# Channel mix of an RWKV layer in six blocks of 512 tokens instead of eight of 384, with one pool of 4 KB buffers and a new plan

## Chip, core and metric

One NeuronCore of a Trainium2 chip runs the whole program. The metric is the time of one execution on the device in microseconds (us). Engines are named as in the profile: PE is TensorE (PEld its weight loads), DVE is VectorE, ACT is ScalarE, POOL is GpSimd, SP is SyncE, whose queue issues every DMA here.

## The reference, cut to what matters

There are 4 batches of 768 tokens and 8 heads of 48 channels, so 384 channels in all.

```python
for t in range(S):                                   # attention, per batch and head
    y[t] = r[t] @ (state + (u * k[t]) v[t]^T)
    state = w[t][:, None] * state + k[t] v[t]^T
x = y as (batch, 768 tokens, 384 channels)
h = (x^T @ U @ V)^T                                  # token mix: 768 -> rank 32 -> 768, over the tokens of a batch
u = x + h
out = u + max(u @ w_ch1, 0) @ w_ch2                  # channel mix: 384 -> 1536 -> 384, each token by itself
```

The token mix needs every token of a batch. The channel mix needs one token at a time, once the token mix of its batch is there.

## The kernel before, in words

**Recurrence.** Each batch is cut into 6 chunks of 128 tokens, 24 in all (`chunk`, L332). A chunk loads the decays (LW), r and k with channels on the partitions (LRK), v (LV) and, after the first batch, r and k with tokens on the partitions (LKR). VectorE scans the decays (F L370, Q L383, with the reciprocal R between them); r and k are scaled by them (RP L390, KS L395, on VectorE or GpSimd). TensorE makes the scores (AM L503), VectorE merges them with the diagonal (CP L506; the diagonal comes by RK L416, RU L419, RED L423 and SEL L433 or L435; in batch 0 by PR L451, MD L457 and DV). TensorE then makes the output (YA L571 and L581, YZ L594 and L598) and adds to the state (DS L513; ZA L542 and ZM L551 carry it on). For DS, k has to be turned: for chunks 0 to 11 TensorE turns it (KT L485) and ScalarE copies it back (KN L494); for chunks 12 to 23 VectorE turns it in 32x32 blocks (KD, L626 by `turn_blocks`, four steps of four instructions). In the same way x is turned for the token mix: by TensorE and ScalarE (XT L654, XN L658) for chunks 0 to 17, by VectorE (XD, L626) for chunks 18 to 23. `TURN_K_DVE` and `TURN_X_DVE` (L36) name the chunks.

**Weights.** `split_raw` (L240) brings 27 pieces of U, V, w1 and w2 in as 64-bit words and turns each into a high and a low fp32r part: AB and E on ScalarE, C1, C2, C3 on VectorE (L286, L293, L300), ADD on GpSimd (L307), then HI and SUB (L317, L324).

**Token mix** (`token_mix`, L666) waits for all six turned chunks of a batch: GA L676, G4, SELM L687, GS, GSL L696.

**Channel mix.** `make_u` (L713) adds the token mix (HP L726 on TensorE, UADD L730 on VectorE) and splits u into high and low (UH L735, UL L741). `ffn` (L759) runs over blocks of `TB` = 384 tokens, two to a batch, eight in all. For each block there are 12 UP steps (L774), each nine matmuls into one PSUM buffer (high and low weight on high u, high weight on low u, for three channel tiles), and after each the split HH (L781 or L783) and HL (L787). Then come 12 DN steps (L810) of nine matmuls, four for each of three output tiles, the sum O (L825) on VectorE and the store OUT (L829). The whole FFN is 8 x 24 x 9 = 1,728 matmuls with 384 columns.

**Buffers.** Hidden activations have a pool of their own (24 tiles of 1.5 KB per partition, 12 pairs), so have the raw weight pieces, which share theirs with u (7), `rk` (4), `kr` (2) and `A` (2). PSUM has three one-bank buffers for the channel mix (`psF`).

**Order.** The steps run in the order of a planner's string, `ORDER` (L53): three digits name a step, its engine where it has two, and a number of leading matmuls (`lead`, L185: bf16 matmuls of 384 columns on constants, issued ahead of the step's own). Each engine's queue holds its steps in this order. `caps` (L219) tells `plan` how many buffers of each pool may be held at one time.

```python
    caps = dict(w=W_BUFS, rk=RK_BUFS, kr=KR_BUFS, v=2, F=2, Q=1, A=2, dv=2, kn=2, Z=2, tr=1, aps=1, y=1, dS=1, ffn=3, xT=3, xn=NCH,
                hid=12, raw=RAW_BUFS, turning=TURNING, cva=CVA_BUFS, g4=1, gs=1, qd=1)
```

Of the kernel before, what the change touches and what calls it, by code (L numbers as in the profile page):

```python
# [27 lines left out]
TB = 384  # L28
RANK = 32
# [10 lines left out]
def channel_order():  # L40
# [49 lines left out]
    "0Fz0Je0F+0F-0Gw0JC0Gt0Jg0Gx0Gu0Ft1Gy0Gv1G+0Ct0Gz1G-"  # L90
    "0Cr0H00K30Cu0Cs0H10Jf0Jv0Cv0KP0Jw1Cw0Jx0J+1KQ1Jy0Cz0Cx0Jz1KR0K60Cy0C+0KS0G00K70G30K80G11C-"
    "0G40K90G50D00G20G60D10D20G90G71G80Ga0GA0IH0GB0II0Il0IJ0Im0Ja1JO0GC0JD0KN0IK0In0Jb0JE1Jh0GF0GD0Io0Ji0GG0KU0JF"
    "0KZ0GH0JG0Ip0K41Ju0GI0Jj0JH0Iq0K50Jl0JI0GJ0Jm0GK0Ka0KO0Ir0KA0Kb1KT0GL0JJ0GE0Gb0GM0JK0GN0GO0JL0KB0GR0GP0GQ0Jk"
    "0GU0IL0GS1Gc0GT0GV1GW0GX0Kc0GY0GZ0KC0Kd0Gd0KD0KE0Gg0Ge0Gf0Gh0Gi0Gj0Gm0Gk0Gl0Gn0H20H50H30H40Go0H61H70Gp0H80Gq"
    "0Gr0HB0H90HA0HE0HC1Jn0Jo0HH0HD0Jp0HK0HF1HI0Jq0KF0HG0HL0HJ0HM0KG0Jr0HN0KH0KI0HQ0HO1KJ0HT0HP0HR0KK0HW0HS0HU1KL"
    "0HZ0HX0HV0HY0Ke0Ha0Hb0Kf0Kl0Kg0Hc0Kh0Ki0Hd0Kj0He0Kk0Km0Hf0Kn0Hi0Hg0Hh0Ko0Hj0Kp0Kq0Kr0Kv0Hk0Ks0Kw0Kt0Kx1Ku0Kz"
    "0Hl0K+0Ky1K-0L00Ho0Hm0Hn0Lt0Lx0Hp0Lu0Ly0Lv0Lw1Lz0L10L+1L-"
    "0Hq0L21M00L30M10Hr0M20L40Hs0Ht0L70L51L60LA0L81L90Lb0LB1LC0LD0LG0LE1LF0LJ0LH0LI0LM0LK1LL0Lc0LN0LO0LP0LS0LQ0LR"
    "0LV0LT1LU0LY0LW1LX0Ld0LZ1La0Le0Lh0Lf0Lg0Li0Lj0Lk0Ln0Ll0Lm0Lo0Lp0M30M60M40M50Lq0M71M80M90Lr0Ls0MC0MA1MB0Md0MD"
    "0ME0MF0MI0MG0MH0ML0MJ0MK0Me0MM1MN0MO0MR0MP1MQ0MU0MS0MT0MX0MV1MW0Ma0MY0MZ0Mf0Mb0Mc0Mg0Mj0Mh0Mi0Mk0Ml0Mm0Mp0Mn"  # L100
    "0Mo0Mq0Mr0Ms0Mt0Mu0"
# [52 lines left out]
def rwkv_moe_kernel(ctx, tc, wT, rkT, vN, rkN, uB, uT, uD, U, V, w1, w2, out):  # L154
# [9 lines left out]
    hidp = pool("hidp", 24)  # L164
# [20 lines left out]
    def lead(to):  # L185
        if leading[0]:
# [32 lines left out]
    caps = dict(w=W_BUFS, rk=RK_BUFS, kr=KR_BUFS, v=2, F=2, Q=1, A=2, dv=2, kn=2, Z=2, tr=1, aps=1, y=1, dS=1, ffn=3, xT=3, xn=NCH,  # L219
                hid=12, raw=RAW_BUFS, turning=TURNING, cva=CVA_BUFS, g4=1, gs=1, qd=1)  # L220
# [802 lines left out]
```

## Time and profile before

| what | value |
|---|---|
| median of 3 runs (lowest, highest) | 488.96 us (488.14, 490.3) |
| profiled execution: its span, from the first to the last instruction | 488.5 us |
| PE busy, share of the span | 456.0 us, 93% |
| DVE busy | 372.3 us, 76% |
| ACT busy | 178.6 us, 37% |
| POOL busy | 120.3 us, 25% |
| DMA moved | 47.38 MB, mean 97 GB/s |
| mean granted TensorE clock | 0.959 |

The profile gives no time for the profiled execution other than its span; the span lies within the runs and 0.5 us under their median. Busy time of an engine is the union of its instructions. In the digit rows of the page, each digit is the busy share of one fortieth of the span in tenths. A matmul's record lasts longer than the distance from one matmul to the next, since matmuls overlap in the array; the pace is the distance between starts.

### The profile page before, as it was taken

What the parts mean: (1) busy time and instruction counts of PE and PEld (TensorE: products, weight loads), DVE (VectorE), ACT (ScalarE), POOL (GpSimd) and SP (SyncE); (2) the same over time, 40 slices, a digit from 0 to 9 for tenths busy, and PEclk for the clock granted to TensorE, in tenths of its full rate; (3) what the DMA queues carried; (4) which work ended last, traced back from release to release, by engine and by line L of the source; (5) the groups of instructions that cost most, each with busy time, mean ns of one, the idle gap of its engine ahead of it and who ended that gap; (6) DMA issues with size and microseconds to landing.
All of it is one profiled execution on the core that took longest, in us unless ns stands there. A gap on an engine that the chain in (4) does not pass through costs nothing.

```text
span 488.5 us, 9955 instructions
## 1 busy us (share of the span) xinstructions
PE 456.0 (93%) x4003; PEld 410.9 (84%) x4003; DVE 372.3 (76%) x768; ACT 178.6 (37%) x471; POOL 120.3 (25%) x110
## 2 busy tenths in 40 slices
PE   7489898899999998999999999999999999999994
PEld 3368665888999977999998779988998899999994
DVE  7798999899989999999998799899328654413410
ACT  5576878466352733445232631150002120100100
POOL 2526533543355262650400312020000010000000
PEclk9656898999999999999999999999999999999999
DMA  8743786327033674134230700030000000000001
GB/s 283 231 153 109 260 286 208 116 88 238 17 102 93 194 222 156 44 115 117 83 109 27 243 23 17 32 96 7 26 25 0 1 34 17 1 33 17 1 17 38
DMA packets 20645, 47.38 MB, mean 97 GB/s; under 512 B 2480, under 2 KB 8880, under 8 KB 20592
## 3 DMA queue, kind: packets, MB, share of 16 engines
q1 hardware_dynamic: 20592, 46.67, 30.0%
q8 instruction: 33, 0.54, 0.5%
q14 instruction: 20, 0.16, 0.1%
HBM read 41.94 MB, written 4.72 MB: 96 GB/s over the span
## 4 chain that ended last, share of the span: by engine, by line
PE 42%; DVE 42%; issue 5%; DMA 4%; ACT 2%; SPq 0%; DVEq 0%; ACTq 0%
PE f L774 17%; PE f L810 15%; DVE kn L626 9%; DVE Q L383 4%; DVE F L370 3%; DVE xn L626 3%; DVE A L506 3%; DVE hl L787 3%; PE aps L503 2%; DVE cva_w L300 1%; DVE xT L730 1%; DVE xT L825 1%; DVE rk L395 1%; DVE dv L423 1%; DVE hh L783 1%
## 5 line engine op out<-in xcount | busy, mean ns | idle before, releaser
L774 PE MATMUL f<-u,w1h 128*128 128x384 f32 x576 | 158.5, 343 | 5.1 <-DVE hl L787 4.1
L774 PEld LDWEIGHTS f<-u,w1h 128*128 128x128 f32 x576 | 105.4, 188 | 10.5 <-DVE hl L787 7.3
L810 PE MATMUL f<-hh,w2h 128*128 128x384 f32 x288 | 100.0, 347 | 0.0
L774 PE MATMUL f<-u,w1l 128*128 128x384 f32 x288 | 97.6, 339 | 0.0
L810 PE MATMUL f<-hh,w2l 128*128 128x384 f32 x288 | 97.5, 338 | 0.0
L781 ACT ACTIVATE hh<-f 128x384 fp32r<-128x384 f32 x61 | 29.9, 490 | 151.9 <-PE f L774 151.6
L787 DVE SCALAR_TENSOR_TENSOR hl<-f,hh 128x384 fp32r<-128x384 f32 x96 | 51.9, 552 | 31.9 <-ACT hh L781 30.6
L810 PE MATMUL f<-hl,w2h 128*128 128x384 f32 x288 | 66.6, 339 | 0.3 <-DVE hl L787 0.3
L810 PEld LDWEIGHTS f<-hh,w2h 128*128 128x128 f32 x288 | 54.1, 188 | 3.6 <-issue 2.8
L810 PEld LDWEIGHTS f<-hh,w2l 128*128 128x128 f32 x288 | 54.1, 188 | 0.4
L774 PEld LDWEIGHTS f<-u,w1l 128*128 128x128 f32 x288 | 54.1, 188 | 0.1
L810 PEld LDWEIGHTS f<-hl,w2h 128*128 128x128 f32 x288 | 51.9, 188 | 0.6 <-DVE hl L787 0.6
L626 DVE STREAM_TRANSPOSE kn<-rk 32x128 f32<-32x128 f32 x160 | 48.3, 302 | 2.5
L433 ACT ACTIVATE A<-ident,dv 128x128 f32<-128x128 f32 x124 | 39.3, 389 | 9.3 <-PE y L581 5.4
L307 POOL TENSOR_TENSOR cva_w<-cva_w,raw_w 128x384 int32<-128x384 int32 x24 | 31.5, 1322 | 40.0 <-DVE cva_w L300 14.0
L825 DVE TENSOR_TENSOR xT<-f,xT 128x384 f32<-128x384 f32 x24 | 13.3, 554 | 35.6 <-PE f L810 35.4
L506 DVE COPY_PREDICATED A<-maskf,aps 128x1024 f32<-128x1024 uint32 x24 | 31.4, 1310 | 5.6 <-PE aps L503 3.2
L741 POOL TENSOR_TENSOR u<-xT,u 128x384 fp32r<-128x384 f32 x12 | 12.1, 1016 | 88.2 <-ACT u L735 88.2
L370 DVE TENSOR_TENSOR_SCAN F<-w,resets 128x517 f32<-128x517 f32 x24 | 31.7, 1331 | 0.9 <-DMA w<-in_wT 0.6
L503 PE MATMUL aps<-rk 48*128 48x128 f32 x384 | 30.9, 305 | 1.4 <-issue 0.9
L503 PEld LDWEIGHTS aps<-rk 48*128 48x128 f32 x384 | 25.9, 205 | 6.4 <-issue 4.8
L383 DVE TENSOR_TENSOR_SCAN Q<-w,qd 128x516 f32<-128x516 f32 x24 | 30.6, 1274 | 0.1
(118 smaller groups left out, 613.4 us busy)
## 6 DMA issues: line engine op xcount, KB each, us to landing
rk<-in_rkT SPq DMA_DIRECT2D x24, 512.0 KB, 4.8
raw_w<-in_w SPq DMA_DIRECT2D x24, 384.0 KB, 4.2
kr<-in_rkN SPq DMA_DIRECT2D x18, 384.0 KB, 3.7
w<-in_wT SPq DMA_DIRECT2D x24, 258.5 KB, 2.7
v<-in_vN SPq DMA_DIRECT2D x24, 224.0 KB, 3.1
out_dram<-xT SPq DMA_DIRECT2D x24, 192.0 KB, 1.9
raw_V<-in_V SPq DMA_DIRECT2D x6, 96.0 KB, 5.2
raw_U<-in_U SPq DMA_DIRECT2D x1, 192.0 KB, 5.5
```

The costliest lines, as they stand in the source:

```text
L307: lambda: nc.gpsimd.tensor_tensor(out=d["to"].bitcast(I32), in0=d["a"].bitcast(I32), in1=d["e"], op=ALU.add),
L370: nc.vector.tensor_tensor_scan(out=F[:, ::-1], data0=st["w"][:, ::-1], data1=resets[:, ::-1], initial=1.0, op0=ALU.mult, op1=ALU.add)
L383: nc.vector.tensor_tensor_scan(out=st["Q"], data0=st["w"][:, 0:n], data1=qd, initial=0.0, op0=ALU.mult, op1=ALU.add)
L433: nc.scalar.activation(A[:, i, j], ident, AF.Copy, scale=dv[:, NP * i + j : NP * i + j + 1])
L503: nc.tensor.matmul(aps[:, i, j, :], rk[r, 1, j, :], rk[r, 0, j, :], start=True, stop=True)
L506: nc.vector.copy_predicated(flat(st["A"]), mask8, flat(st["aps"]))
L626: nc.vector.transpose(to[32 * j : 32 * j + 32, :, 32 * i : 32 * i + 32], src[32 * i : 32 * i + 32, :, 32 * j : 32 * j + 32])
L774: nc.tensor.matmul(ps, wt[:, f, ct, :], u[ct][:, z], start=(n == 0), stop=(n == 8))
L781: nc.scalar.activation(hh, d["ps", f], AF.Relu)
L787: nc.vector.scalar_tensor_tensor(out=hl, in0=d["ps", f], scalar=0.0, in1=hh.bitcast(F32), op0=ALU.max, op1=ALU.subtract)
L810: nc.tensor.matmul(d["o", ct], wt[:, 4 * ct + part, f - 3 * part, :], hid[f][z], start=(part == 0 and n == 0), stop=(part == 3 and n == 8),)
L825: nc.vector.tensor_tensor(out=o, in0=d["o", ct], in1=o, op=ALU.add)
```

## The change

The channel mix works on blocks of `FB` = 512 tokens, numbered through all batches: `NB` = 6. Blocks 1 and 4 lie across a border between batches, so their HP step is two matmuls, each with its batch's token mix (`segments`), and they need the token mix of both batches. `gs` has two buffers. Block 0 and no other can run before the second batch's token mix is there; before, blocks 0.0 and 0.1 could. The output in DRAM has the batch behind the partition, so that a block is stored as one stretch. The channel mix becomes 6 x 24 x 9 = 1,296 matmuls with 512 columns.

Raw weights, `rk`, `kr`, `A`, u and the hidden activations (high and low in one tile) share one pool of 20 buffers of 4 KB per partition. The two lists of chunks that VectorE turns are empty, so all turns of k and x are KT and XT on TensorE with KN and XN on ScalarE. `ORDER` is new.

```diff
-RAW_BUFS, TURNING, CVA_BUFS, KR_BUFS, W_BUFS, RK_BUFS = 7, 4, 3, 2, 2, 4
-TURN_K_DVE, TURN_X_DVE = range(12, 24), range(18, 24)
+FB = 512
+NB = B * S // FB
+CPB = FB // P
+BIG_BUFS, TURNING, CVA_BUFS, W_BUFS = 20, 4, 3, 2
+TURN_K_DVE, TURN_X_DVE = (), ()
 ORDER = (
...
-    hidp = pool("hidp", 24)
+    big = pool("big", BIG_BUFS)
...
-    caps = dict(w=W_BUFS, rk=RK_BUFS, kr=KR_BUFS, v=2, F=2, Q=1, A=2, dv=2, ..., hid=12, raw=RAW_BUFS, ..., gs=1, qd=1)
+    caps = dict(big=BIG_BUFS, w=W_BUFS, v=2, F=2, Q=1, dv=2, ..., gs=2, qd=1)
...
             def mix(ct=ct):
-                hp = d["hp", ct] = psF.tile([P, TB], F32, tag="ffn", name=f"hp_{b}_{blk}_{ct}")
+                hp = d["hp", ct] = psF.tile([P, n], F32, tag="ffn", name=f"hp_{blk}_{ct}")
                 lead(hp)
                 cs = slice(ct * P, (ct + 1) * P)
-                nc.tensor.matmul(hp, gs["gs"][:, cs], Vst[:, ts], start=True, stop=True)
+                for b, t, w in segs:
+                    nc.tensor.matmul(hp[:, at : at + w], gss[b]["gs"][:, cs], Vst[:, t : t + w], start=True, stop=True)
+                    at += w
...
-                hh = hidp.tile([P, TB], F32R, tag="hid", name=f"hh_{b}_{blk}_{f}")
-                hl = hidp.tile([P, TB], F32R, tag="hid", name=f"hl_{b}_{blk}_{f}")
+                h = hid[f] = big.tile([P, 2, n], F32R, tag="big", name=f"hid_{blk}_{f}")
...
-        for blk in range(2):
-            make_u(b, blk)
-            ffn(b, blk)
+        for blk in range(NB):
+            segs = segments(blk)
+            if segs[-1][0] == b:
+                make_u(blk, segs, ...)
+                ffn(blk, lambda ct, blk=blk: flat[ct, :, blk * FB : (blk + 1) * FB])
```

The two order strings, read step by step, give these counts. The first UP step is `UP 0.0.0` before and `UP 0.1` after; the second batch's mix begins with `HP 1.0.0` before and `HP 1.0` after.

| stretch of the plan | engine | before | after |
|---|---|---|---|
| up to the first UP | DVE | F 8, R 8, Q 8, C1 14, C2 13, C3 12, PR 5, SUB 9, RP 7, KS 3, RK 1, RU 2, RED 3, CP 7, ZA 4, T 4, DV 3, ZM 2, HI 1, GSL 1, UADD 3, UL 3 | F 10, R 9, Q 8, C1 14, C2 13, C3 13, PR 6, SUB 10, RP 6, KS 8, RK 3, RU 3, RED 3, CP 7, ZA 4, GSL 1, UADD 3, UL 3 |
| up to the first UP | POOL | 25 steps | 16 steps |
| from there to the second batch's first HP | DVE | F 8, R 7, Q 7, C1 13, C2 14, C3 15, SUB 12, RP 2, KS 6, RK 6, RU 5, RED 8, CP 6, ZA 4, T 4, HI 2, KD 7, HL 24, HH 6, UADD 3, UL 3, O 5, GSL 1 | F 3, R 4, Q 5, C1 11, C2 12, C3 11, SUB 9, RP 3, KS 5, RK 4, RU 2, RED 4, CP 5, ZA 4, T 3, HI 2, HL 12, O 1, GSL 1 |
| from there to the second batch's first HP | PE | UP 24, DN 21, AM 6, YA 6, YZ 5, DS 5, XT 5, KT 4, HP 3, GA 2, SELM 1 | UP 12, DN 7, AM 4, YA 5, YZ 5, DS 4, XT 5, KT 4, GA 2, SELM 1 |
| from there to the second batch's first HP | POOL | 40 steps | 19 steps |
| from the first UP to the end | PE, without UP and DN | AM 17, YA 17, YZ 15, DS 14, XT 11, KT 4, GA 6, SELM 3, HP 21 | AM 16, YA 17, YZ 15, DS 14, XT 17, KT 13, GA 6, SELM 3, HP 15 |
| whole plan | DVE | 562 steps | 454 steps |
| whole plan | leading matmuls | 91: 11 at the first UP, 15 at the eleventh UP, the other 65 earlier | 43, all before the first UP |

In the plan after, the last three VectorE steps counted up to the first UP (one C1, one SUB, one F) stand behind or beside the last UL. Buffers of the common pool that are held at one time reach the limit of 20 at 79 of the 1,301 places of the plan, all of them between block 0's UP steps and block 2's last.

## Rows read from the trace of the kernel before

**Rows 1.** From the page: the span, the busy time of each engine, VectorE's busy tenths and TensorE's granted clock, in 40 slices of the span.

```profile
span 488.5 us, 9955 instructions
...
PE 456.0 (93%) x4003; PEld 410.9 (84%) x4003; DVE 372.3 (76%) x768; ACT 178.6 (37%) x471; POOL 120.3 (25%) x110
...
DVE  7798999899989999999998799899328654413410
...
PEclk9656898999999999999999999999999999999999
```

**Rows 2.** Busy time of each engine in four stretches: up to the first UP matmul, on to the second batch's mix, on to the last chunk's scores, and on to the last matmul.

```profile
core 0: us, PE busy (x) PEld busy (x) DVE busy (x) ACT busy (x) POOL busy (x), PEclk, DMA share, GB/s
0.00:84.30 84.30, 68.89 (x746) 49.25 (x747) 74.23 (x128) 58.84 (x163) 35.45 (x32) 0.78 0.67 216
84.30:191.80 107.50, 101.85 (x958) 93.13 (x956) 102.11 (x190) 54.40 (x140) 45.64 (x40) 1.00 0.44 139
191.80:342.60 150.80, 146.87 (x1410) 134.08 (x1410) 137.97 (x321) 51.54 (x141) 36.15 (x35) 1.00 0.25 77
342.60:481.90 139.30, 138.26 (x894) 134.47 (x893) 57.47 (x129) 13.84 (x28) 3.07 (x3) 1.00 0.05 17
```

**Rows 3.** The chain of work that ended last: its shares by engine from the page, and its two longest pieces in order of time (start, length, what).

```profile
PE 42%; DVE 42%; issue 5%; DMA 4%; ACT 2%; SPq 0%; DVEq 0%; ACTq 0%
...
427.95 14.31 PE f L810 x81
...
466.11 15.92 PE f L810 x90
```

**Rows 4.** What one matmul takes: the leading bf16 matmuls by line (duration ns min/median/max), a run of eleven of them on the timeline (start, length), and two weight loads of UP from the timeline behind it, where TensorE had stood idle.

```profile
L183 PE MATMUL f<-resets x26: 326/326/337, 82.7 to 104.2; 128*128 128x384 bf16 x26
...
102.55 1.95 PE L183 MATMUL f<-resets 128*128 128x384 bf16 x11
...
104.49 0.19 PEld L774 LDWEIGHTS f<-u,w1l 128*128 128x128 f32 x1
104.60 0.19 PEld L774 LDWEIGHTS f<-u,w1h 128*128 128x128 f32 x1
```

**Rows 5.** VectorE's groups of instructions by line and shape over the whole span (busy us, mean ns of one), and for two of them the durations by line (ns min/median/max).

```profile
L626 DVE STREAM_TRANSPOSE kn<-rk 32x128 f32<-32x128 f32 x160 | 48.3, 302 | 2.5
L626 DVE STREAM_TRANSPOSE xn<-xT 32x96 f32<-32x96 f32 x96 | 25.9, 270 | 3.8 <-ACT xT L614 2.4
L787 DVE SCALAR_TENSOR_TENSOR hl<-f,hh 128x384 fp32r<-128x384 f32 x96 | 51.9, 552 | 31.9 <-ACT hh L781 30.6
L370 DVE TENSOR_TENSOR_SCAN F<-w,resets 128x517 f32<-128x517 f32 x24 | 31.7, 1331 | 0.9 <-DMA w<-in_wT 0.6 <-ACT xT L614 0.2
L383 DVE TENSOR_TENSOR_SCAN Q<-w,qd 128x516 f32<-128x516 f32 x24 | 30.6, 1274 | 0.1
L506 DVE COPY_PREDICATED A<-maskf,aps 128x1024 f32<-128x1024 uint32 x24 | 31.4, 1310 | 5.6 <-PE aps L503 3.2 <-ACT A L433 2.1
L416 DVE TENSOR_TENSOR kr<-kr 128x384 f32<-128x384 f32 x8 | 8.1, 1013 | 0.4 <-DMA kr<-in_rkN 0.3
L390 DVE TENSOR_TENSOR rk<-rk,Q 128x512 f32<-128x512 f32 x14 | 12.2, 868 | 1.6 <-DMA rk<-in_rkT 1.6
...
L416 DVE TENSOR_TENSOR kr<-kr x8: 547/1204/1368, 60.6 to 283.1; 128x384 f32<-128x384 f32 x8
...
L390 DVE TENSOR_TENSOR rk<-rk,Q x14: 673/685/1664, 14.7 to 330.5; 128x512 f32<-128x512 f32 x14
```

**Rows 6.** The timeline shortly before the first UP: three UADD steps that overlap at their ends, the UL step that ends channel tile 0 of u, and TensorE's leading matmuls, behind which the first UP matmul starts at 84.31.

```profile
77.82 1.49 DVE L730 TENSOR_TENSOR xT<-hp,xT 128x384 f32<-128x384 f32 x3
...
81.63 0.53 DVE L741 TENSOR_TENSOR u<-xT,u 128x384 fp32r<-128x384 f32 x1
...
82.66 1.95 PE L183 MATMUL f<-resets 128*128 128x384 bf16 x11
```

**Rows 7.** TensorE's timeline where steps of the chunks stand back to back: AM, YA (its first half), YZ (its first half), XT, the next AM, later DS, GA and the next YZ; and, from an earlier stretch, one KT between two steps of the channel mix. The price of a step is the distance from its start to the next step's.

```profile
265.01 1.16 PE L503 MATMUL aps<-rk 48*128 48x128 f32 x16
266.10 0.65 PE L571 MATMUL y<-A,v 128*32 128x128 f32 x16
...
267.00 0.62 PE L594 MATMUL y<-rk,Z 128*32 128x128 f32 x16
...
267.76 0.55 PE L654 MATMUL trx<-ident,xT 128*128 128x128 f32 x3
268.24 1.16 PE L503 MATMUL aps<-rk 48*128 48x128 f32 x16
...
270.82 0.56 PE L513 MATMUL dS<-v,kn 128*48 128x48 f32 x16
271.31 0.85 PE L676 MATMUL ga<-xn,U_sb 128*32 128x384 f32 x8
271.99 0.62 PE L594 MATMUL y<-rk,Z 128*32 128x128 f32 x16
...
149.25 0.60 PE L485 MATMUL trk<-ident,rk 128*128 128x128 f32 x4
149.60 0.42 PE L810 MATMUL f<-hh,w2h 128*128 128x384 f32 x1
```

**Rows 8.** The end of the chain of work (start, length), and the landing time of a chunk's r and k (KB each, median us from issue to landing).

```profile
482.12 0.56 DVE xT L825
...
rk<-in_rkT SPq DMA_DIRECT2D x24, 512.0 KB, 4.8
```

More of the change, by code (lines that the diff above doesn't have):

```diff
@@ L428, in diag @@
             if i == 0:
[L429 removed]
+                st["A"] = big.tile([P, 2, NP, P], F32, tag="big", name=f"A_{g}")
             A, dv = st["A"], st["dv"]
@@ L628, in turn_blocks, with turn @@
             )
-    def turn(b, c, after, bx, bxn):
-        blk, cc = divmod(c, TB // P)
+    def turn(b, c, blk, cc, after, bx, bxn):
         btr = Buf("tr")
@@ L711, in rwkv_moe_kernel, with make_u @@
     ub, ups = {}, []
-    def make_u(b, blk):
-        d = ub[b, blk] = dict(bufs=[Buf("raw") for _ in range(NCT)], uhs=[], uls=[], u={})
-        gs = gss[b]
-        bx = xbuf[b, blk]
+    def make_u(blk, segs, xs):
+        n = sum(w for _, _, w in segs)
+        d = ub[blk] = dict(n=n, bufs=[Buf("big") for _ in range(NCT)], uhs=[], uls=[], u={})
+        bx = xbuf[blk]
+        mixes = [gss[b] for b, _, _ in segs]
+        vs = [s for i in range(2) for s in ready.get(("V", i), [])]
         hp = None
@@ L741, in low @@
                 ENG[eng].tensor_tensor(
-                    out=u[:, 1], in0=blocks[b, blk][:, ct, :], in1=u[:, 0].bitcast(F32), op=ALU.subtract
+                    out=u[:, 1], in0=blocks[blk][:, ct, :], in1=u[:, 0].bitcast(F32), op=ALU.subtract
                 )
-            nm = f"{b}.{blk}.{ct}"
+            nm = f"{blk}.{ct}"
             hp = step(
-                "HP " + nm, "PE", mix, [gs["step"], hp] + ready.get(("V", blk), []), take=[bhp], use=[gs["buf"]],
+                "HP " + nm, "PE", mix, [m["step"] for m in mixes] + [hp] + vs, take=[bhp], use=[m["buf"] for m in mixes],
             )
-            xs = [s for c in range(3 * blk, 3 * blk + 3) for s in xns[b, c]["steps"] + xs_done.get((b, c), [])]
             ad = step("UADD " + nm, "DVE", add, [hp] + xs, use=[bhp, bx])
@@ L800, in ffn @@
             for part in range(4):
-                nm = f"{b}.{blk}.{ct}.{part}"
+                nm = f"{blk}.{ct}.{part}"
                 fs = range(3 * part, 3 * part + 3)
@@ L812, in down @@
                             wt[:, 4 * ct + part, f - 3 * part, :],
-                            hid[f][z],
-                            start=(part == 0 and n == 0),
-                            stop=(part == 3 and n == 8),
+                            hid[f][:, z],
+                            start=(part == 0 and m == 0),
+                            stop=(part == 3 and m == 8),
                         )
@@ L912, in general @@
             for c in range(NCH):
-                turn("g", c, [], xbuf["g", c // 3], Buf("xn"))
+                n, cc = divmod(c, TB // P)
+                turn("g", c, halves[n], cc, [], xbuf[halves[n]], Buf("xn"))
             token_mix("g")
-            dst = out[bass.ds(b, 1)].rearrange("o c p t -> (o c) p t")
-            for blk in range(2):
-                make_u("g", blk)
-                ffn("g", blk, dst=dst)
+            to = out[:, :, bass.ds(b, 1)].rearrange("c p o t -> c (p o) t")
+            for n, blk in enumerate(halves):
+                make_u(blk, [("g", n * TB, TB)], [s for c in range(NCH) for s in xns["g", c]["steps"]])
+                ffn(blk, lambda ct, n=n: to[ct, :, n * TB : (n + 1) * TB])
             for s in steps:
```

207 lines of the change are left out of this document (103 added, 104 removed).

## The prediction

> **What bounds the kernel now.** I read the page first. TensorE is busy 93% of the span, but VectorE's digits stand at 8 and 9 for two thirds of it, and only then fall [rows 1]. The chain of waits is shared evenly, 42% and 42%, and its long unbroken TensorE pieces all lie at the end [rows 3]. So I cut the span into stretches [rows 2]. Up to the first UP (84.3 us) VectorE is busy 74.2. From there to 191.8 it is busy 102.1 of 107.5 (95%), on to 342.6 it is busy 138.0 of 150.8. After that it is under half busy and TensorE alone sets the time. VectorE paces 342.6 us, TensorE the last 139.3.
>
> TensorE's share can be booked by steps. A run of the channel mix goes at 15.92 / 90 = 0.1769 and 14.31 / 81 = 0.1767 us a matmul [rows 3], so 1,728 take 305.3. The chunks' steps cost, start to start [rows 7], AM 1.09, YA 0.90, YZ 0.76, XT 0.48, DS 0.49, GA 0.68 (its second part, with half the chunks, half of that); KT 0.35 and 0.09 more behind it, 0.44. With SELM put like GA's first part and HP at a matmul's pace, the steps after the first UP (17 AM, 17 YA, 15 YZ, 14 DS, 11 XT, 4 KT, three mixes, 21 HP) make 68.0. From 84.3 to TensorE's end near 481.8 are 397.5, so 24.2 are left in which TensorE waits, 2.3 of them on the 15 leading matmuls ahead of the eleventh UP. In the last 139.3 there are 729 matmuls of the channel mix (128.8) and some 7.5 of other steps, so only 3.0 us of waiting, 2.2%. Nearly all of the waiting lies where VectorE paces. The span is then
>
> 84.3 front + 305.3 channel mix + 68.0 other steps + 24.2 waiting + 6.7 end = 488.5.
>
> The profile's own execution has this span and no other time; the median of the runs, 488.96, lies 0.5 above it. A measurement can tell about 0.5%, 2.4 us, from no change.
>
> **The channel mix: 1,296 matmuls of 512 columns.** No fp32r matmul of 512 columns is in the trace, so I bound it. Below: the bf16 matmuls of 384 columns have (1.95 - 0.326) / 10 = 0.1624 us [rows 4]; by columns that is 0.2165 for 512. Above: all of 0.1767 grows with the columns, 0.2356. Between them, if the 0.0143 that fp32r costs over bf16 is fixed for each matmul, 0.2308. Is the pace perhaps that of the weight loads, which bigger blocks would spread? A load lasts 0.19, longer than the pace, but where TensorE had stood idle two loads start 0.11 apart [rows 4], so loads could follow faster than matmuls do. I take columns as the limit and the middle of the two upper values, 0.233: 302.0 us, a gain of 3.3 (bounds -0.0 and -6.2 by the two nearer values; 24.7 by the lowest).
>
> By the Trainium skill, "TensorE: Matmul & The Clock Gate", section "Back-to-back issue gap", a warm matmul takes its columns at 2.4 GHz plus 2.5 ns; that is 162.5 ns for 384, which the bf16 rows bear out and the fp32r rows (176.7) do not. By that rule 512 columns would take 215.8 ns and the channel mix 279.7 us.
>
> **All turns on TensorE.** VectorE loses 160 and 96 block transposes, 48.3 + 25.9 = 74.2 us [rows 5], all but 28 of them behind the second batch's mix. TensorE gets after the first UP 9 KT (4.0) and 6 XT (2.9); an AM less there (-1.1) and 5% fewer HP columns (-0.2) make 73.6 of 68.0. ScalarE gets the copies, and at 37% [rows 1] it hides them; without that cover each would cost a copy of one turn.
>
> **VectorE's wider steps.** HL, HH, UADD, UL, O take 0.55 for 384 columns; another operation with 512 has a median of 0.685 [rows 5], which I use. A quarter fewer steps at 1.24 times the time: 7% less on those.
>
> **The front.** From the counts of the plans: up to the first UP, VectorE gets F twice more (2.7), KS five and PR one (5.2 at RP's mean), RK two (2.0), R, SUB, C3 and RU one each (2.0), wider UADD and UL (0.8), and loses an RP (0.9) and ten T, DV, ZM, HI (some 0.3 each, an estimate between F's and the shortest rows; 3.1): 8.7 more. Three of the last (2.4) don't gate the UP. Rows overlap at their ends (three of 0.55 in 1.49 [rows 6]), and 372.3 busy is 0.936 of all counts by means, so 5.9 us. Against that, the first UP's matmuls stood ready behind 11 leading ones: UL ended at 82.16, UP began at 84.31 [rows 6]; without them 1.6 us less. First UP: 84.3 + 5.9 - 1.6 = 88.6. The shorter leading stretch (43 leading matmuls up to the first UP for 76) may leave the clock low, which is 0.78 in the front now [rows 2]; I put that into the range.
>
> **The second batch's mix.** Block 0 alone has to cover it: 19 UP and DN steps (39.8) and the chunk steps of the table (20.6), 60.4 of TensorE. It would be through at 149.0. VectorE: before, 176.3 busy up to there [rows 2]. From the counts go 3 F (4.0), 2 Q (2.5), 1 CP (1.3), 28 block transposes (8.5), HL, HH, UADD, UL, O (16.6 + 6.6 + 2.8 become 8.2 + 4.1 + 0.7: 13.0), 28 smaller steps at some 0.42 (an estimate between a short step and HL; 11.8), and 5 KS and PR come (4.3): 36.8, times 0.936 is 34.4. With 30 GpSimd steps fewer (65 to 35), VectorE's steps are disturbed less: L416 and L390 last 1.01 and 0.87 on the mean and 0.55 and 0.67 at least [rows 5], 6.5 us in all over 103 GpSimd steps, 1.9 for 30. So 140.0 busy, plus the front's 10.1 idle and 5% of the next 67 (3.4): 153.5. TensorE waits 4.5 us in the first block.
>
> **From there on** TensorE has 315.2 of steps (302.0 + 73.6 - 60.4). VectorE has the lighter load, the transposes being gone, so I let TensorE wait as it does now where it sets the time, 2.2%: 6.9. The last output tile's sum and store are wider: 0.69 for 0.56 [rows 8], and a third more bytes, together 0.4: end 7.1.
>
> 88.6 + 302.0 + 73.6 + 11.4 + 7.1 = **482.7** of span, so 483.2 for the runs. What pays is that waiting shrinks from 24.2 to 11.4; the steps as such are 2.3 longer, the front 4.3.
>
> **Rivals.**
>
> *The waiting comes back through the common pool (slower).* Before, a chunk's `rk`, `kr` and `A` had eight buffers that the channel mix could not take. Now hidden activations and u hold 15 of 20 in every block, released only by the last output tile, and the plan stands at the limit in the middle of the run. A load that waits for such a release blocks SP's queue for the loads behind it, and lands 4.8 us after its issue [rows 8]. At five block borders that is 24 us; if DN steps cover half, 12 us: 494.7 of span. It decides from 5.8 us of added waiting on, little more than one bare landing. For it: VectorE and TensorE both hang on those loads. Against it: the third and fourth batch's chunks have slack now, since VectorE has 74 us less to do.
>
> *The front grows (no change).* TensorE's steps behind the first UP are as long as before, so each us that the front loses is lost. VectorE idles 10.1 in the front now [rows 2]; with 16.0 the first UP comes at 94.5 and the span is 488.6. For it: more is done ahead, by fewer GpSimd steps, with less warming. Against it: the same chain of six chunks.
>
> *512 columns at bf16's pace (faster).* If the 0.0143 us is not paid at 512, because it is the price of a load not hidden, the channel mix takes 1,296 x 0.2165 = 280.6, 21.4 less: 461.3. Against it: the loads 0.11 apart. By the skill's rule named above it would be 22.3 less, 460.4.
>
> **How the numbers follow.** I give the forecast 0.50, the pool 0.24, the front 0.18, the faster pace 0.08. The forecast's own range is 476 to 489 for the runs: matmul pace -2.7 to +3.4, front and first block 4 us either way. To leave no more than 2 in 10 out, it reaches into the pool's case and part way to the faster pace: 469 to 495.5. Faster by over 0.5%: 0.44 of the forecast's chance, the 0.08, and 0.04 of the front's: 0.56. Within 0.5%: 0.05 of the forecast, 0.12 of the front and 0.03 of a mild pool case: 0.20. Slower: 0.24.
>
> **What the changed profile would show.** The starts of successive UP matmuls 0.233 apart (0.2165: the faster rival). First UP near 89, the second batch's HP near 153, and TensorE without a gap over 1 us behind it. VectorE's busy total near 372 - 74 - 3 = 295, its digits below 9 after the second batch's mix. TensorE's waits named for `rk`, `kr` or DMA, or SP's queue waiting on DN's matmuls, would speak for the pool. A first UP beyond 94 or more than 11 us of waiting behind it makes the prediction wrong.

## The result, and the profile after

| | before | after |
|---|---|---|
| median of the runs beside each other (lowest, highest) | 489.32 us (488.14, 490.3), 4 runs | 466.48 us (465.2, 467.25), 4 runs |
| ratio, 95% interval | | 0.9525 (0.9489 to 0.9561) |
| span of the profiled execution | 488.5 us | 463.4 us |

The change saves 22.8 us. The prediction had 483.2 and a range from 469.0: right in sign, far too small in size. Booked by the prediction's own terms (the first UP at 77.7, 1,296 matmuls at 0.2333, the same step prices, TensorE's end at 456.6):

| term, us | before | predicted | after |
|---|---|---|---|
| front, up to the first UP | 84.3 | 88.6 | 77.7 |
| channel mix | 305.3 | 302.0 | 302.4 |
| other steps | 68.0 | 73.6 | 73.6 |
| waiting (what remains) | 24.2 | 11.4 | 2.9 |
| end | 6.7 | 7.1 | 6.8 |
| sum | 488.5 | 482.7 | 463.4 |

Channel mix and end came as forecast; the other steps are booked at the forecast's prices, so the table does not test them. The front missed by 10.9 us, the waiting by 8.5.

From the page after (answers to [rows 1]): span, busy times, VectorE's busy tenths, TensorE's clock.

```profile
span 463.4 us, 8789 instructions
...
PE 441.2 (95%) x3581; PEld 347.1 (75%) x3581; DVE 284.8 (61%) x468; ACT 187.9 (41%) x508; POOL 93.0 (20%) x88
...
DVE  7899999899899897728586535435514151133210
...
PEclk9568899999999999999999999999999999999999
```

Busy times by stretch after (answers to [rows 2]): the front, block 0 up to the second batch's mix, and on.

```profile
core 0: us, PE busy (x) PEld busy (x) DVE busy (x) ACT busy (x) POOL busy (x), PEclk, DMA share, GB/s
0.00:77.70 77.70, 62.15 (x734) 44.98 (x734) 72.02 (x131) 60.89 (x179) 20.57 (x23) 0.82 0.76 255
77.70:136.00 58.30, 58.30 (x613) 46.14 (x612) 53.92 (x100) 44.01 (x117) 19.22 (x18) 1.00 0.42 133
136.00:200.00 64.00, 64.00 (x551) 51.64 (x550) 53.41 (x84) 29.62 (x79) 22.22 (x21) 1.00 0.43 133
200.00:300.00 100.00, 100.00 (x843) 79.50 (x845) 56.95 (x81) 30.78 (x87) 26.94 (x23) 1.00 0.26 84
300.00:342.60 42.60, 42.60 (x366) 33.56 (x359) 18.43 (x28) 10.67 (x27) 2.76 (x2) 1.00 0.04 13
342.60:456.60 114.00, 114.00 (x490) 91.30 (x488) 29.40 (x48) 11.98 (x21) 1.30 (x1) 1.00 0.05 17
```

Two things are to be seen. Behind the first UP, TensorE is busy in every stretch for its whole length; before, the three stretches had 5.65, 3.93 and 1.04 us of idle time, 10.6 in all [rows 2]. And the front has three VectorE instructions more than before (131 for 128) and yet less VectorE time, 72.0 for 74.2, beside 20.6 us of GpSimd work for 35.4.

The chain after (answers to [rows 3]), its shares, two long pieces of the channel mix and its end (which answers to [rows 8]):

```profile
PE 83%; DVE 6%; ACT 4%; DMA 3%; issue 1%; SPq 1%; DVEq 0%
...
382.95 12.60 PE f L804 x54
...
408.15 21.00 PE f L770 x90
...
456.81 0.69 DVE xT L819
```

VectorE's share of the chain fell from 42% to 6%. 12.60 / 54 and 21.00 / 90 are both 0.2333 us a matmul: the forecast's 0.233, not the 0.2165 of the faster rival. By the rule of the Trainium skill that the prediction names (215.8 ns) they would be 7.5% shorter; the trace does not agree for fp32r.

The last VectorE and TensorE work before the first UP (answers to [rows 6]; start, length): UADD and UL follow one another without a gap, and three leading matmuls and one KT end as the first UP starts.

```profile
73.39 1.89 DVE L726 TENSOR_TENSOR xT<-hp,xT 128x512 f32<-128x512 f32 x3
75.19 1.89 DVE L737 TENSOR_TENSOR u<-xT,u 128x512 fp32r<-128x512 f32 x3
```

```profile
76.82 0.65 PE L175 MATMUL trk<-resets 128*128 128x384 bf16 x3
77.30 0.60 PE L477 MATMUL trk<-ident,rk 128*128 128x128 f32 x4
77.66 0.48 PE L770 MATMUL f<-u,w1h 128*128 128x512 f32 x1
```

Durations of RK and RP by line after (ns min/median/max; they answer to the last two of [rows 5]):

```profile
L409 DVE TENSOR_TENSOR kr<-kr x10: 527/556/1499, 33.5 to 216.5; 128x384 f32<-128x384 f32 x10
...
L383 DVE TENSOR_TENSOR rk<-rk,Q x13: 664/686/843, 10.5 to 240.4; 128x512 f32<-128x512 f32 x13
```

RK's median was 1,204 ns before, now 556; RP's longest was 1,664, now 843. The work is the same.

### The profile page after: what moved, and what is told of

The parts are those of the page before. It is cut to its first block, busy times and chain, and to the rows that moved or that the text cites. A ratio compares the mean times of both kernels' runs of the same rounds, so it can differ in the third digit from the quotient of the medians.

```text
span 463.4 us, 8789 instructions
## 1 busy us (share of the span) xinstructions
PE 441.2 (95%) x3581; PEld 347.1 (75%) x3581; DVE 284.8 (61%) x468; ACT 187.9 (41%) x508; POOL 93.0 (20%) x88
## 4 chain that ended last, share of the span: by engine, by line
PE 83%; DVE 6%; ACT 4%; DMA 3%; issue 1%; SPq 1%; DVEq 0%
PE f L770 33%; PE f L804 33%; PE aps L495 4%; DMA raw_w<-in_w 3%; PE y L563 2%; PE trx L645 2%; PE y L573 2%; PE trk L477 2%; ACT A L426 1%; PE dS L505 1%; PE y L586 1%; PE ga L667 1%; PE hp L721 1%; DVE Q L376 1%; DVE F L363 1%
## 5 line engine op out<-in xcount | busy, mean ns | idle before, releaser
L770 PE MATMUL f<-u,w1h 128*128 128x512 f32 x432 | 145.1, 401 | 0.0
L804 PE MATMUL f<-hid,w2h 128*128 128x512 f32 x432 | 142.1, 398 | 0.0
L770 PEld LDWEIGHTS f<-u,w1h 128*128 128x128 f32 x432 | 81.2, 188 | 19.8 <-issue 1.2
L804 PEld LDWEIGHTS f<-hid,w2h 128*128 128x128 f32 x432 | 81.2, 188 | 19.6 <-DVE rk L383 0.6
L770 PE MATMUL f<-u,w1l 128*128 128x512 f32 x216 | 85.5, 396 | 0.0
L804 PE MATMUL f<-hid,w2l 128*128 128x512 f32 x216 | 85.5, 396 | 0.0
L775 ACT ACTIVATE hid<-f 128x512 fp32r<-128x512 f32 x49 | 28.8, 595 | 121.4 <-PE f L770 118.0
L781 DVE SCALAR_TENSOR_TENSOR hid<-f,hid 128x512 fp32r<-128x512 f32 x72 | 48.3, 684 | 46.9 <-ACT hid L775 46.5
L804 PEld LDWEIGHTS f<-hid,w2l 128*128 128x128 f32 x216 | 40.6, 188 | 9.1
L498 DVE COPY_PREDICATED A<-maskf,aps 128x1024 f32<-128x1024 uint32 x24 | 31.7, 1319 | 12.5 <-PE aps L495 11.1
L777 DVE TENSOR_SCALAR hid<-f 128x512 fp32r<-128x512 f32 x23 | 15.8, 685 | 32.8 <-PE f L770 32.6
L726 DVE TENSOR_TENSOR xT<-hp,xT 128x512 f32<-128x512 f32 x18 | 12.1, 688 | 14.8 <-PE hp L721 14.7
```

The lines of the kernel that those rows point to most:

```text
L498: nc.vector.copy_predicated(flat(st["A"]), mask8, flat(st["aps"]))
L770: nc.tensor.matmul(ps, wt[:, f, ct, :], u[ct][:, z], start=(m == 0), stop=(m == 8))
L775: nc.scalar.activation(h[:, 0], d["ps", f], AF.Relu)
L777: nc.vector.tensor_scalar(out=h[:, 0], in0=d["ps", f], scalar1=0.0, scalar2=None, op0=ALU.max)
L781: nc.vector.scalar_tensor_tensor(out=h[:, 1], in0=d["ps", f], scalar=0.0, in1=h[:, 0].bitcast(F32), op0=ALU.max, op1=ALU.subtract)
L804: nc.tensor.matmul(d["o", ct], wt[:, 4 * ct + part, f - 3 * part, :], hid[f][:, z], start=(part == 0 and m == 0), stop=(part == 3 and m == 8),
```

## The experiments

Times are medians; the ratio to the kernel before stands with its interval. "Remainder" is the time from the first UP to TensorE's end less the channel mix: 92.3 us before (68.0 + 24.2, rounded), 76.5 after.

### Which engine turns (e1, e9, e2)

e1: the changed kernel with the k of chunks 12 to 23 and the last batch's x turned on VectorE, the four steps of a turn together (ten of these chunks turn k, since a batch's last chunk adds nothing to the state). e9: the same, spread among VectorE's other steps.

```diff
-TURN_K_DVE, TURN_X_DVE = (), ()
+TURN_K_DVE, TURN_X_DVE = range(12, 24), range(18, 24)
-ORDER: KT 12 ... KT 22, XT 3.0 ... XT 3.5
+ORDER: in their places four KD or XD each
```

> The changed kernel with the turns of chunks 12 to 23 (k) and of the fourth batch (x) put back on VectorE, at the places where TensorE had them. TensorE loses 10 KT and 6 XT (7.3 us), VectorE gets 74.2 us of block transposes. Theory A (VectorE's load made TensorE wait; that is gone because VectorE is lighter): TensorE, which waits for next to nothing behind 136 us now, waits again; VectorE has some 77 us free between 136 and 343 us, so it is nearly full: span 463 - 7 + 10 to 20 = 466 to 476 us. Rival B (the turns were beside the point; blocks, pool and plan made the gain): TensorE's 7.3 us come off and the span is near 456 us.

Measured: 517.95 us (ratio 1.0564, 1.0513 to 1.0614), 51 us above the changed kernel and far above both expectations. Stretches of e1:

```profile
136.00:200.00 64.00, 53.48 (x424) 42.09 (x423) 56.15 (x111) 24.17 (x67) 18.21 (x17) 0.92 0.31 97
200.00:260.00 60.00, 51.31 (x410) 40.86 (x410) 43.47 (x92) 10.30 (x26) 13.24 (x14) 0.91 0.31 101
260.00:320.00 60.00, 46.05 (x384) 34.75 (x383) 46.34 (x114) 14.13 (x44) 10.89 (x11) 0.89 0.16 52
```

And its longest group of TensorE's waits (in all, times, longest):

```profile
PE f L771 <- DVE hid L782: 17.8, 5, 5.8
```

VectorE is busy under 90% of every stretch, and TensorE still stands: UP waits up to 5.8 us for one HL, which stands behind turn steps in VectorE's queue; in all, turn steps fill 24.7 of the 41.1 us in which TensorE has nothing to do behind the first UP. And the clock, 1.00 behind the first UP in the changed kernel, has a mean of 0.89 to 0.92 in these stretches: after it had stood idle, TensorE ran a part of the time at the lower of its two levels (1.2 and 2.4 GHz).

> As the first experiment, turns of k from chunk 12 on and of the fourth batch's x on VectorE in the changed kernel, but the four steps of each turn are spread over VectorE's steps between the place where TensorE turned and the first reader, so that no other step stands behind 1.2 us of transposes at once. If the 518 us of the first experiment came of the clumped places, this gives 466 to 485 us; if VectorE's load and the two engines' waiting for each other make it, it stays over 495 us, with VectorE under 90% busy and TensorE's granted clock below 1.0 in the stretches where it waits.

Measured: 505.98 us (1.0305, 1.0259 to 1.0352). Spreading gives back 12 of 51 us; the rest stays, at a clock of 0.91 to 0.94. The changed order has no room for these steps in VectorE's queue.

e2: the kernel before with all turns on TensorE.

```diff
-TURN_K_DVE, TURN_X_DVE = range(12, 24), range(18, 24)
+TURN_K_DVE, TURN_X_DVE = (), ()
```

> The kernel before with all turns on TensorE and nothing else changed (order kept, each KT and KN, XT and XN at the place of the block transposes). TensorE gets 7.3 us of steps, VectorE loses 74.2 us behind 132 us. Theory A: of the waiting, 11 us lie between 84 and 192 us, where few turns are, and 10 us between 192 and 343 us; most of the latter goes: 488.5 + 7.3 - 8 to 12 = 484 to 488 us, so the turns alone are worth 0 to 1%. Rival B: TensorE's waiting stays: 496 us. A third reading, that the turns alone carry the whole gain, needs 470 us or less.

Measured: 487.48 us (0.9962, 0.9937 to 0.9987). VectorE's busy time fell from 372 to 303 us, and the time by 2. The remainder is 90.2, of which 75.3 are steps: waiting fell from 24.2 to 14.9, and 7.3 us of new TensorE steps took nearly all of it. The turns alone bring little.

### The front (e3, e8, e4, e5)

e3: eight KS, PR, RK and RU steps of the changed front back on GpSimd. e8: 21 KS, RP, RK and RU steps between the first UP and the third block's mix to GpSimd.

```diff
-ORDER: KS 0, KS 3, KS 4, KS 5, PR 1, RK 7, RK 8, RU 8 on DVE
+ORDER: the same steps on POOL
```

> The changed kernel with eight steps of the front given back to GpSimd, about the ones that GpSimd has there in the kernel before (KS of chunks 0, 3, 4, 5, PR 1, RK 7 and 8, RU 8). VectorE loses 5.2 us of steps at their undisturbed lengths. Theory C (VectorE's two-operand steps stretch while GpSimd works, so the front was shortened by taking steps off GpSimd): VectorE's other steps grow again, its busy time up to the first UP stays within 2 us of 72, and the first UP comes at 78 to 83 us, span 464 to 469. Rival D (a step costs the same wherever GpSimd stands; the front is shorter by its new order): VectorE's busy time falls to 67 us and the first UP comes at 73 to 76 us, span 459 to 462.

Measured: 468.17 us (0.9544, 0.9496 to 0.9591); first UP 80.7. Its front:

```profile
0.00:80.70 80.70, 68.47 (x732) 50.10 (x733) 73.56 (x123) 61.22 (x179) 31.63 (x31) 0.75 0.72 246
```

VectorE has eight steps fewer and is busy 1.5 us longer. The instructions' durations add up to 82.2 us for 81.6: the eight steps (5 us by the shortest rows) came back as longer steps elsewhere, some 0.7 us for each step moved. The first UP itself says little: other kernels with the changed kernel's front have it as late as 80.3 (e8).

> The changed kernel with 21 steps of the first two blocks (KS, RP, RK, RU between the first UP and the third batch's first HP) given to GpSimd instead of VectorE, some 14 us of VectorE's steps at undisturbed lengths. Theory C (GpSimd's work stretches VectorE's): VectorE's busy time between 77.7 and 200 us falls by less than 7 us from 107, the steps that stay get longer; TensorE waits somewhat, 466 to 475 us of span. Rival D: VectorE's busy time falls by 13 us or more, and as TensorE has no waiting left to lose there, the span stays at 463 to 465.

Measured: 467.12 us (0.9526, 0.9485 to 0.9567). In 122.3 us behind the first UP VectorE is busy 102.6 for 107.3. The durations add up to 113.3 us for 120.2: 6.9 less, where 21 steps left that take 12.5 by the shortest rows, so 5.6 / 21 = 0.3 us were given back for each. TensorE never waited.

e4: nine such steps of the front before from GpSimd to VectorE.

```diff
-ORDER: KS 0, KS 3, KS 4, KS 5, PR 1, RP 3, RK 7, RK 8, RU 8 on POOL
+ORDER: the same steps on DVE
```

> The kernel before with nine steps of the front moved from GpSimd to VectorE (KS of chunks 0, 3, 4, 5, PR 1, RP 3, RK 7 and 8, RU 8) and nothing else. At undisturbed lengths they are 5.9 us more for VectorE. Theory C: VectorE's other steps get shorter by as much or more; busy time up to the first UP 70 to 75 us (74.2 now), first UP at 80 to 85 us (84.3 now), span 484 to 489. Rival D: VectorE busy 80 us, first UP at 89 to 90 us, span 493 to 495.

Measured: 488.93 us (0.9974, 0.9946 to 1.0003), first UP 83.2 for 84.3. Nine steps more, and the durations add up to 85.3 for 83.1: VectorE pays 2.2 us for some 5.6 us of work by the shortest rows, so (5.6 - 2.2) / 9 = 0.4 us given back for each.

e5: the kernel before without 38 leading matmuls.

```diff
-ORDER: leading matmuls at XT 1.0, UP 0.0.0 and UP 0.0.10
+ORDER: none there
```

> The kernel before without the 38 leading bf16 matmuls at XT 1.0 (12), at the first UP (11) and at the eleventh UP (15); they write nothing that is used. Theory E: those at the first UP and at XT 1.0 hold the front back (u was ready at 82.2 us, UP began at 84.3), those at the eleventh UP hold TensorE for 2.3 us: 488.5 - 3 to 5 = 483 to 486 us of span. Rival: without them the granted clock falls as UP begins and UP's first steps run at the low level: no gain, 487 to 492 us.

Measured: 488.71 us (0.9977, 0.9945 to 1.0009). The first UP came 2.6 us sooner than in the kernel before (though e2 and e12, with its front, have it 2.2 and 1.4 sooner too), the remainder grew by 3.4, and the clock stood at 0.93 for the first 50 us behind it (1.00 before): no gain, as the rival had it.

### Blocks or order (e7, e10, e11, e12)

e7: the kernel before with e2's and e5's edits, and 23 KS, PR, RP, RK and RU steps up to the second batch's mix from GpSimd to VectorE. Blocks of 384, pools and order stay.

```diff
-ORDER: 23 steps ahead of HP 1.0.0 on POOL
+ORDER: the same steps on DVE
```

> The kernel before with three parts put together: all turns on TensorE, no leading matmuls at those three places, and all KS, PR, RP, RK and RU steps that GpSimd has up to the second batch's mix (23) on VectorE; blocks stay at 384 tokens, pools and order as before. The turns alone gave a span of 484.0. Theory F (waiting on VectorE, GpSimd's disturbance and the leading matmuls make most of the 25 us, whatever the block size): 470 to 477 us. Rival G (the rest needs the new blocks, pool or order): the parts add up to little, 478 to 484 us; VectorE stays the pace up to 192 us.

Measured: 487.47 us (0.9968, 0.9935 to 1.0001). First UP 80.1, remainder 93.4, 18 of it waiting; the span, 485.2, lies even above rival G's range. These parts together do not make the change; blocks, pool and order are left.

e10: the changed kernel with blocks of 384.

```diff
-FB = 512
+FB = 384
-BIG_BUFS = 20
+BIG_BUFS, SMALL_BUFS = 7, 17
```

> The changed kernel with the channel mix back in eight blocks of 384 tokens (which then lie within a batch). The order of all other steps, the engines, the turns and the token mixes stay those of the changed kernel, the channel mix's steps stand at the same share of its work, and w2's splits are moved forward in proportion, since the first DN step comes earlier. The buffers are cut anew from the same memory: 7 of 4 KB and 18 of 3 KB. Theory P (the new order and the engines took the waiting away): the same front (76 to 81 us), 1,728 x 0.1767 = 305.3 of channel mix, some 76.5 of other steps, 2 to 6 of waiting, 6.8 at the end: 467 to 475 us. Theory B (the larger blocks took it away: longer UP and DN steps leave VectorE more time for the halves of each, and w2's splits longer to come): the waiting of 12 to 18 us comes back, mostly in the first 30 us behind the first UP: 479 to 488 us.

Measured: 510.7 us (1.0419, 1.0376 to 1.0461), outside both. TensorE idles 27 us behind the first UP, with VectorE busy 58% of the span. It doesn't tell the theories apart: an order that was stretched to other blocks fits neither, and the buffers changed with it (7 of 4 KB and 17 of 3 KB, not the 18 of the expectation, and a fourth one for x).

So I put the steps behind the first UP in a new order for blocks of 384, by their durations in these traces: e11 with e7's steps, e12 with those of the kernel before.

```diff
-ORDER: from UP 0.0.0 on as in the kernel before
+ORDER: from UP 0.0.0 on each step where its engine is free and its inputs are there
```

> The kernel before with all turns on TensorE, no leading matmuls at the three places, 23 early steps on VectorE (as in e7, 487.5 us) and, new, the steps behind the first UP put in another order on every engine. Blocks of 384 tokens, their 1,728 matmuls, the buffers and the steps themselves stay as before. Theory O (most of the waiting that e7 kept, some 18 us, lies in the order of the queues): it falls to 3 to 8, the span to 470 to 476, the runs to 471 to 477. Theory B (it lies in blocks of 384 tokens, whose UP steps of 1.6 us leave too little time for the halves of each): the waiting stays at 14 to 18 and the time at 482 to 488.

Measured: 487.36 us (0.9959, 0.9933 to 0.9986), theory B's side. First UP 79.6, remainder 94.0. From 140 us on TensorE has no idle time, as in the changed kernel; the first 60 us are different:

```profile
80.00:110.00 30.00, 25.99 (x151) 24.62 (x151) 29.34 (x57) 17.63 (x40) 10.85 (x10) 0.88 0.51 154
110.00:140.00 30.00, 26.39 (x265) 24.00 (x264) 29.39 (x50) 15.23 (x35) 10.98 (x8) 1.00 0.32 102
```

VectorE is busy 98% there and TensorE idles 7.6 us. The changed kernel has 53.9 of 58.3 and none in its first block. The longest group of TensorE's waits for VectorE in e11's stretch is this (in all, times, longest):

```profile
PE f L766 <- DVE u L733: 2.7, 2, 2.1
```

These are the UL of block 0. In the front, which e11 has from the kernel before, the three UL stand apart behind other steps of VectorE (they start at 81.1, 82.4 and 83.7 us, with the first UP at 79.6); in the changed kernel they follow one another and are through before the first UP. So 2.7 of the 7.6 us lie in the order of the front, which e11 did not change.

> The kernel before with the steps behind the first UP put in another order, and nothing else changed: turns on VectorE, 65 GpSimd steps up to the second batch's mix, the leading matmuls, blocks of 384 tokens. If order alone makes the waiting (theory O), it falls from 24 us to 5 to 10 and the time to 470 to 477. If VectorE's load is what TensorE waits for (busy 95% of 84 to 192 us before, as the prediction had it), 15 to 25 us of waiting stay and the time is 481 to 490. Against the re-planned kernel with all turns on TensorE the difference of the two is what moving the turns is worth once the order fits: 0 to 5 us by the first, 10 or more by the second.

Measured: 511.06 us (1.0461, 1.0406 to 1.0516), outside both. TensorE waited 12.1 us for HL in nine waits, the longest 4.9. The turns are mostly not what stood in front of it there: turn steps fill 3.1 of the 26.3 us in which TensorE has nothing to do behind the first UP, and none of the longest wait, in which VectorE did RK, RU, KS and F. This order is a poor one for these steps; what the turns cost in a good order, and what order alone is worth, e12 does not show.

### Why the first block of 384 waits (e13, e14)

A block of 384 uses all 24 pieces of w1 and w2 within 24 x 9 x 0.1767 = 38 us, one of 512 within 50. In the 59 us behind the first UP VectorE did C3 for 15 pieces in e11 (one of them V's), for 11 in the changed kernel. e13 is e11, e14 the changed kernel, each without C1, C2 and C3 of w2, so that w2's values are no longer the reference's.

```diff
-            lambda: nc.vector.tensor_scalar(
+            lambda: kind == "w2" or nc.vector.tensor_scalar(
```

> As e11 (blocks of 384, all turns on TensorE, behind the first UP in a new order; 487.4 us), without VectorE's steps C1, C2 and C3 of the twelve pieces of w2 (36 steps of 0.35, 0.35 and 0.55 us at least, 15 us in all; w2's values are then not split as the reference's). Theory S (the first block of 384 waits for VectorE's splits): TensorE's 7.6 us of idle time between 80 and 140 us fall below 2 and the clock there goes up, the time falls by 7 to 12 us, to 475 to 481. Rival (it waits for the halves of the hidden activations, step by step, whatever else VectorE does): the time falls by less than 3 us, to 485 to 487.

Measured: 480.58 us (0.9813, 0.9763 to 0.9863), 6.8 below e11, as theory S had it:

```profile
80.00:110.00 30.00, 26.85 (x164) 25.25 (x163) 24.53 (x41) 18.79 (x44) 12.91 (x13) 0.94 0.47 152
110.00:140.00 30.00, 30.00 (x301) 28.35 (x300) 24.72 (x43) 17.31 (x42) 7.83 (x7) 1.00 0.36 114
```

The idle time fell from 7.6 to 3.2 (below 2 was expected), and the clock of the first 30 us rose from 0.88 to 0.94. The waits for UL stay (2.3 for 2.7); the others fell from some 5 us to 1. So TensorE waited for VectorE's load there. That it must be splits is not shown: no other 15 us of VectorE's steps were taken away, and in e11 only 0.5 us of TensorE's idle time was a wait of DN for a split weight.

> The changed kernel (blocks of 512; 466.5 us) without the same 36 steps of w2's splits on VectorE. TensorE had no idle time behind the first UP, so by theory S nothing is to be had there: 465 to 467, with VectorE's busy time 13 to 17 us lower, and the front within its usual 2 us, as hardly any of w2 is split ahead of the first UP. If the time falls by 3 us or more, VectorE still paced some of the changed kernel.

Measured: 464.84 us (0.9522, 0.9483 to 0.9561). VectorE is busy 9.8 us less (13 to 17 expected), the remainder is the changed kernel's 76.5, and the 1.6 us gained lie in the first UP, 75.9 for 77.7, which differs by as much between kernels of the same front. Cutting the same VectorE work speeds up blocks of 384 and leaves the waiting of blocks of 512 as it is: none.

### A lighter front (e6)

```diff
-ORDER: leading matmuls at HP 0.0 and KT 7; KS 7, R 8 ahead of UADD; AM 7, KT 7 ahead of UP 0.1
+ORDER: no leading matmuls there; KS 7, R 8 behind UL 0.2; AM 7, KT 7 behind UP 0.1
```

> The changed kernel without its leading matmuls at the first mix's first HP and at KT 7, and with KS 7 and R 8 on VectorE behind the last UL of block 0, AM 7 and KT 7 on TensorE behind the first UP: fewer steps ahead of the first UP. If the front is a sum of VectorE steps and each us ahead of the first UP counts, the first UP comes some 2 us sooner and the time is 1.5 to 2.5 us lower, 464 to 465. If the leading matmuls hold the clock up and the moved steps are only paid for behind the first UP, where VectorE has 4 us of idle time in 58, the time stays within 1 us of the changed kernel's 466.5.

Measured: 465.5 us (0.9497, 0.9464 to 0.953), 1.0 below the changed kernel, with overlapping intervals. First UP 76.6 (-1.1, within what equal fronts differ by), remainder 78.9 (+2.4): the moved steps were paid for behind the first UP. No version here beats the changed kernel by more than can be told.

## Why the prediction was wrong

**Channel mix and end: right.** The pace was bounded by 0.2165 and 0.2356, taken as 0.233 and measured as 0.2333. The bounds were worked out; that the middle of the upper two came so close is in part luck. The booked step prices left a remainder that fits to 3 us.

**The front: the step that failed first.** It priced VectorE's new steps at the means of the trace before and put nine GpSimd steps fewer in the front at nothing. It gave 80.1 us busy and 8.5 idle; the trace has 72.0 and 5.7. Only for the stretch up to the second batch's mix was there a credit, 0.063 us for each of 30 GpSimd steps, and it came from two of VectorE's groups alone, RK and RP (6.5 us over 103). e3, e4 and e8 put it at 0.3 to 0.7 us for each step, four to eleven times as much. Nine GpSimd steps fewer in the front are then worth 3 to 6 of the 8.1 us; the means themselves carried the same stretch into the price of the new steps (RK was priced at 1.01 us, and its median is 0.556 now). I had both ends in [rows 5], the shortest and the mean, and took the mean.

The traces show it. In the kernel before, the seven RP beside which GpSimd stood still took 682 ns on the mean and the seven beside which it worked 1,055; for RK it is 555 (three) and 1,288 (five). C1, C2, C3, KS, SUB and the scans F and Q were longer beside GpSimd's work too, which the prediction left out. What VectorE's steps took beyond the usual length of their own line and shape adds up to 9.7 us in the front before and 1.7 after: 8.0 less, the size of the miss.

By the Trainium skill, "GPSIMD Engine Reference", section "1. Specifications", GpSimd shares its memory interface with VectorE and gets in the way of VectorE instructions that read two operands from SBUF or run in a two-port mode. The traces agree: RP, with two such operands, took up to 1,664 ns before [rows 5], while HL, which reads one operand from PSUM, was never stretched. Whether C1 and C2, which read one operand, run in such a mode the traces do not say. HL's durations by line in the kernel before (ns min/median/max):

```profile
L787 DVE SCALAR_TENSOR_TENSOR hl<-f,hh x96: 523/557/559, 86.9 to 466.7; 128x384 fp32r<-128x384 f32 x96
```

**The second batch's mix: the same step, carried on.** VectorE was to have been busy 140.0 us up to there and to be through at 153.5; it was busy 128.5, and TensorE's HP came at 138.8:

```profile
0.00:138.80 138.80, 123.25 (x1358) 93.34 (x1359) 128.46 (x235) 107.24 (x301) 40.83 (x42) 0.90 0.62 204
```

The stretch of VectorE's steps up to there was 20.0 us before and 4.5 after, where the prediction took off 1.9. It also added 10.1 us of idle time in the front, where its own sum of the front leaves 8.5. TensorE's 4.5 us of waiting in the first block were 0.

**The waiting: misread, then mis-sized.** The 24.2 us were a remainder, and I called them waiting; [rows 2] show 10.6 us of idle time, and 2.3 were the leading matmuls. The others were matmuls spaced further apart than the prices say, at step borders and behind stops, where the records overlap and no gap shows: counted from start to start, idle time included, the channel mix took 321.7 us (305.3 booked) and the other steps without the leading matmuls 73.4 (68.0). In the changed kernel it is 308.0 (302.4) and 70.7 (73.6). I then let 2.2% (6.9 us) go on behind the second batch's mix by analogy with the last stretch before. There the changed kernel has none.

**What pays.** The prediction let VectorE's lost turns do it. e2 shows 9 us less waiting by them and 7 us more steps. In the changed kernel's order they are needed all the same, since e1 and e9 lose 39 to 51 us by putting them back. e11 and e13 against e14 show the other part: 15 us less of VectorE's steps are worth 6.8 us to blocks of 384, and to blocks of 512 at most 1.6, all of it in the first UP. A likely reason is that a block of 512 uses the same weights in 50 us instead of 38; it is argued, not shown. The changed kernel leads e11 by 22 us of span: 1.9 in the front, 2.9 in the channel mix, 17.5 in the remainder (one KT and one AM of it are steps, 1.5).

**The rivals.** No wait for the pool shows: TensorE has no idle time at any block border. The front shrank instead of growing. The faster pace did not come.

**What stays open.** e13 still has 88.0 - 75.3 = 12.7 us of waiting by this booking, and the changed kernel 2.9. Some 3 us of the difference are idle time in e13's first 30 us. Counted from start to start, e13's channel mix takes 317.4 us and the changed kernel's 308.0: 2.9 is the pace, 4.4 lie in the first 30 us behind the first UP, and some 2 are left for the larger number of step borders (192 for 144) and all else. The other steps take 75.7 us for 70.7, 3.3 more than their prices say. How much of the first 30 us is the front's order, how much VectorE's load and how much the pool was not separated; no run changes the pool alone. An order for blocks of 384 that does as well was not found, which is no proof that there is none.

## What to carry to other kernels

A mean duration from a trace holds the disturbance of that trace: where GpSimd's load changes, price VectorE's steps at their shortest rows and put a price of its own on every GpSimd step, and do not move a step to GpSimd just because it has time to spare. What remains when TensorE's steps are booked is not yet idle time: compare it with the busy rows before you say what it waits for. A bigger block does more than save instructions; it also leaves more time for the weights in the first block (50 us for 38 here), and an order planned for one block size need not fit another: stretched to blocks of 384, the changed kernel's lost 44 us (e10).

## What was not expected of the hardware

- An fp32r matmul's pace is nearly in proportion to its columns, 0.1767 us for 384 and 0.2333 for 512, though its weight load lasts 0.188 us in both: at 384 the load is longer than the pace.
- 74 us of VectorE work taken away were worth 2 us in one order (e2), and put back cost 51 in another (e1).
- The first UP of kernels with the changed kernel's front came at 75.7 (e1), 75.9 (e14), 77.7, 77.9 (e9) and 80.3 us (e8), with the front of the kernel before at 82.1 (e2), 82.9 (e12) and 84.3: differences of 4 us in the front can't be read from one profile, while VectorE's busy time in it (71.8 to 72.5 and 73.2 to 74.6) is steadier.
